# Eight batches of attention and a mixture of experts on one core: the first pair of heads in pieces, low parts on VectorE or GpSimd, and other costs and keys in the planner

## The chip, the cores and the metric

The kernel runs on one core of a Trainium2 chip. The metric is the device time of one execution in microseconds (us). A core has five engines that run beside each other, each with its own instruction stream that is worked off strictly in order: TensorE (PE in the profile, its weight loads PEld), VectorE (DVE), ScalarE (ACT), GpSimd (POOL) and SyncE (SP), which here only issues DMAs. An instruction that waits for a semaphore holds up everything behind it on its engine.

## The reference, cut to what matters

```python
def _attn_ref(q, k, v):                       # (8, 8, 576, 64) each
    ...
    q_rot, k_rot = (rotate(q), rotate(k))     # rotary embedding
    scores = scale * np.matmul(q_rot, k_rot.transpose(0, 1, 3, 2))
    scores = scores - np.max(scores, axis=-1, keepdims=True)
    attn = np.exp(scores)
    attn = attn / (np.sum(attn, axis=-1, keepdims=True) + 1e-09)
    return np.matmul(attn, v).astype(np.float32)

def _moe_ref(x, w_gate, w1, w2, capacity):    # x (8, 576, 512), capacity 128
    scores = np.einsum('bsd,d->bs', x, w_gate)
    out = x.copy()
    for b in range(B):
        top_idx = np.argpartition(-scores[b], capacity)[:capacity]
        xe = x[b, top_idx]
        h = np.maximum(xe @ w1, 0.0)          # 512 -> 1024
        ye = h @ w2                           # 1024 -> 512
        g = 1.0 / (1.0 + np.exp(-scores[b, top_idx]))
        out[b, top_idx] = x[b, top_idx] + g[:, None] * ye
    return out.astype(np.float32)
```

## The kernel before

The 64 heads are worked as 32 pairs, two heads on 64 partitions each; four pairs make a batch. For every pair SyncE loads k and q (640 KB each, every column with its rotated partner beside it) and v. `rotate` multiplies k and q in place by tables of cosines and sines (`tabk`, `tabq`) and adds the two halves, into `rk` and `rq`, 640 columns each: two multiplies of 1280 elements and two adds of 640 for a pair. `tabq` is `tabk` times 1/8, made once by ScalarE. `split_qk` splits each of `rk` and `rq` into a rounded high part (`kh`, `qh`, a cast on ScalarE) and a low part (`kl`, `ql`, the difference, "low part" below), so that three matmuls (kh·qh, kl·qh, kh·ql) give a product of nearly full precision. There is one `rk` and one `rq` for all pairs: the add of the next pair must wait until high and low part of this one are made. `k_in` and `q_in` have two buffers each.

`attend` then makes nine units of scores for a pair (two heads by 4.5 tiles of 128 rows, each 128x576 in PSUM). For each unit VectorE takes the negative row maximum (`nm`), ScalarE the exponential with row sums (`pab`, or `pr` for the last unit), TensorE turns it with transposes, ScalarE or VectorE copies the turned tile to SBUF (`pt`, `pk`), TensorE multiplies with v, and after another transpose VectorE scales the rows into `x`. Every second pair `x` is stored, and GpSimd multiplies it by the gate's weights (`prod`). When a batch is complete, `route` counts ranks on VectorE, picks 128 tokens, GpSimd gathers them, and TensorE puts them through two layers, again with three matmuls for a product. The weights of these layers are loaded in 16 pieces of 256 KB through two stages (`xe`, `row`) during the first batches and split into high (ScalarE) and low parts (GpSimd), the `w` instructions.

The first pair (`first` in `rotate`) is rotated by VectorE, all others by GpSimd. All low parts of k and q are made by VectorE, 640 columns in one instruction (the first pair's q in two pieces).

The order of every engine's stream is set on the host, before the program is built. Each piece of work is an `Op` with a key (when it is wanted) and, for each engine that may do it, how long the engine is taken and when the result is there. `Order.run` plays these Ops forward in time: an engine that is free takes the ready Op with the smallest key, TensorE also with a price for changing between three kinds of matmul (`SWITCH`), and Ops that may run on two engines go to the one that takes them first. The numbers in `KEY` are added to the keys or set limits: `ahead` is how early the split of a pair is wanted, `kstep` how much later its q comes than its k, `load` and `rotate` how early loads and rotations are wanted. An Op of `mode` 2 on VectorE begins in the plan no earlier than GpSimd is free, and GpSimd then waits for it; before the change only ten small gate products at the very end carry that mode there. All instructions go through one helper (`call`, L204 in the profile of before), so the profile's rows are told apart by the names of their tiles.

## Time and profile before

| | before |
|---|---|
| median of 3 runs (lowest to highest) | 676.64 us (676.56 to 678.98) |
| the profiled execution's own time | 677.76 us |
| its span, first to last instruction | 676.0 us |
| PE busy in the span | 622.7 us (92%) |
| DVE, ACT, POOL busy | 537.5, 419.4, 387.6 us |
| mean granted clock of TensorE | 0.988 |

A row of the timeline gives the start and the length in us, the engine, the operation, the tiles written and read, the number of instructions merged, and in brackets how long the engine had been idle before and what released it. A busy time includes the time in which an instruction that has started waits for a port. A row of the groups gives the total busy time in us and the mean of one instruction in ns.

### The profile page before, as it was taken

What the parts mean: (1) busy time and instruction counts of PE and PEld (TensorE: products, weight loads), DVE (VectorE), ACT (ScalarE), POOL (GpSimd) and SP (SyncE); (2) the same over time, 40 slices, a digit from 0 to 9 for tenths busy, and PEclk for the clock granted to TensorE, in tenths of its full rate; (3) what the DMA queues carried; (4) which work ended last, traced back from release to release, by engine and by line L of the source; (5) the groups of instructions that cost most, each with busy time, mean ns of one, the idle gap of its engine ahead of it and who ended that gap; (6) DMA issues with size and microseconds to landing.
All of it is one profiled execution on the core that took longest, in us unless ns stands there. A gap on an engine that the chain in (4) does not pass through costs nothing.

```text
span 676.0 us, 13857 instructions
## 1 busy us (share of the span) xinstructions
PE 622.7 (92%) x5072; PEld 474.5 (70%) x5072; DVE 537.5 (80%) x1294; ACT 419.4 (62%) x998; POOL 387.6 (57%) x260
## 2 busy tenths in 40 slices
PE   1789898999799999999999999999999999999896
PEld 0657676777677776787767777777777777677674
DVE  6978788899978958897787978789687978879451
ACT  3657767777566656676676656766665666757211
POOL 4877879883875656655575765557476533201110
PEclk9989999899999999999999999999999999999999
DMA  9524655331351334233233323322343302001200
GB/s 322 173 87 149 199 169 156 114 97 58 114 171 57 129 112 138 90 111 102 82 113 96 131 79 114 114 94 87 112 148 95 116 19 84 18 2 36 67 17 31
DMA packets 36708, 71.02 MB, mean 105 GB/s; under 512 B 7712, under 2 KB 25120, under 8 KB 36640
## 3 DMA queue, kind: packets, MB, share of 16 engines
q1 hardware_dynamic: 35216, 65.29, 30.2%
q0 software_dynamic: 1280, 4.20, 1.7%
q8 instruction: 40, 0.66, 0.4%
q10 hardware_dynamic: 144, 0.66, 0.3%
q14 instruction: 28, 0.23, 0.1%
HBM read 58.59 MB, written 11.53 MB: 104 GB/s over the span
## 4 chain that ended last, share of the span: by engine, by line
PE 50%; DVE 32%; issue 7%; ACT 4%; POOL 4%; DMA 2%; POOLq 0%; DVEq 0%; ACTq 0%
PE ps L204 50%; DVE nm L204 9%; DVE junk L204 6%; DVE pt L204 3%; ACT pab L204 3%; DVE ql L204 3%; DVE kl L204 2%; DVE x L204 2%; POOL prod L204 2%; DVE sel L204 1%; DVE rs L204 1%; DVE gp L204 1%; DMA k_in<-k_dram 1%; DMA row<-w_dram 1%; DMA xe<-w_dram 1%
## 5 line engine op out<-in xcount | busy, mean ns | idle before, releaser
L204 ACT ACTIVATE pab<-ps,nm 128x576 f32<-128x576 f32 x256 | 188.1, 740 | 122.5 <-DVE nm L204 121.8
L204 DVE TENSOR_REDUCE nm<-ps 128x1 f32<-128x576 f32 x288 | 205.8, 749 | 70.8 <-PE ps L204 68.6
L204 PE MATMUL ps<-ident,pab 128*128 128x128 f32 x1152 | 162.2, 281 | 13.0 <-ACT pab L204 9.0
L204 PEld LDWEIGHTS ps<-ident,pab 128*128 128x128 f32 x1152 | 132.6, 144 | 29.1 <-ACT pab L204 14.2
L204 PE MATMUL ps<-pt,vt 128*64 128x320 f32 (+1 forms) x1024 | 140.3, 417 | 0.4 <-ACT pab L204 0.4
L204 POOL TENSOR_TENSOR k_in<-k_in,tabk 128x1280 f32<-128x1280 f32 x31 | 91.0, 2937 | 50.5 <-DMA k_in<-k_dram 50.5
L204 PE MATMUL ps<-kh,qh 64*128 64x288 f32 (+1 forms) x576 | 85.7, 346 | 22.9 <-ACT qh L204 10.6
L204 ACT COPY pt<-ps 128x512 f32<-128x512 f32 x156 | 89.0, 597 | 25.5 <-PE ps L204 25.2
L204 PEld LDWEIGHTS ps<-pt,vt 128*64 128x64 f32 x1024 | 68.7, 138 | 50.1 <-issue 8.1
L204 POOL TENSOR_TENSOR rk<-k_in 128x640 f32<-128x640 f32 x31 | 60.9, 1964 | 66.6 <-DVE kl L204 54.9
L204 DVE COPY pt<-ps 128x512 f32<-128x512 f32 x132 | 88.3, 680 | 9.7 <-PE ps L204 7.1
L204 PEld LDWEIGHTS ps<-kh,qh 64*128 64x128 f32 (+1 forms) x576 | 49.1, 188 | 65.7 <-ACT pab L204 30.4
L204 POOL TENSOR_TENSOR q_in<-q_in,tabq 128x1280 f32<-128x1280 f32 x31 | 91.3, 2947 | 4.6 <-DMA q_in<-q_dram 4.4
L204 POOL TENSOR_TENSOR prod<-x,wg 128x512 f32<-128x512 f32 (+1 forms) x45 | 52.3, 1163 | 50.4 <-DVE x L204 23.0
L204 PE MATMUL ps<-kh,ql 64*128 64x288 f32 (+1 forms) x576 | 70.3, 297 | 5.5 <-DVE ql L204 5.3
L204 PE MATMUL ps<-kl,qh 64*128 64x288 f32 (+1 forms) x576 | 69.6, 295 | 0.3 <-DVE kl L204 0.3
L204 PEld LDWEIGHTS ps<-kh,ql 64*128 64x128 f32 (+1 forms) x576 | 52.6, 188 | 6.2 <-DVE ql L204 6.2
L204 PEld LDWEIGHTS ps<-kl,qh 64*128 64x128 f32 (+1 forms) x576 | 52.5, 188 | 0.6 <-DVE kl L204 0.6
L204 PE MATMUL ps<-w,xt 128*128 128x512 f32 x192 | 51.7, 409 | 1.2 <-ACT xt L204 0.6
L204 POOL TENSOR_TENSOR rq<-q_in 128x640 f32<-128x640 f32 x31 | 48.2, 1554 | 7.4 <-DVE rs L204 4.3
L204 PE MATMUL ps<-w,ht 128*128 128x512 f32 x192 | 51.3, 406 | 0.5 <-DVE ht L204 0.5
L204 ACT ACTIVATION_READ_ACCUMULATOR pab<-ps,nm 128x1 f32 x256 | 50.6, 198 | 0.0
(94 smaller groups left out, 779.7 us busy)
## 6 DMA issues: line engine op xcount, KB each, us to landing
k_in<-k_dram SPq DMA_DIRECT2D x32, 640.0 KB, 3.9
q_in<-q_dram SPq DMA_DIRECT2D x32, 640.0 KB, 5.3
vt<-v_dram SPq DMA_DIRECT2D x32, 256.0 KB, 3.1
out_dram<-x SPq DMA_DIRECT2D x16, 512.0 KB, 3.6
xe<-w_dram SPq DMA_DIRECT2D x8, 256.0 KB, 3.5
row<-w_dram SPq DMA_DIRECT2D x8, 256.0 KB, 3.4
vr<-v_dram SPq DMA_DIRECT2D x64, 16.0 KB, 2.5
out_dram<-x SPq DMA_DIRECT2D x16, 64.0 KB, 3.2
```

Source lines behind the costliest of these rows:

```text
L204: i = made(*args, **kwargs)
```

## The change

In the first pair, k is cut at column 352 and q at columns 128 and 384 (`KCUTS`, `QCUTS`). Loads, table, rotation, high and low parts are made piece by piece, the pieces of k and q in turn; the table comes in two DMAs on ScalarE's queue, now Ops of the plan. For all later pairs the low parts may be made by VectorE or GpSimd, and so may the low parts of the expert weights. In the plan, VectorE's instructions with two operands in SBUF (rotation and low parts) carry `mode` 2, and such an Op isn't taken by VectorE while GpSimd is busy. Transfers carry their bytes (`moved`) and land one after the other at 350 bytes a ns, plus 1700 ns. Three costs (row sums and reciprocals, the parts of the gate scores, the gather) are set higher, and all numbers in `KEY` but `half` and `hold` are new; two lines of them stand for the rest below.

```diff
-KEY = dict(ahead=5300, lag=11900, rem=120, value=3300, rows=13200, load=22300, rotate=92400, half=2000,
-           gate=15815, route=58400, count=31800, select=12400, turn=17500, step=9176, kstep=2700, hold=2,
...
+KEY = dict(ahead=6669, lag=12977, rem=76, value=4203, rows=388, load=49858, rotate=24073, half=2000,
+           gate=54405, route=49769, count=21851, select=23426, turn=18811, step=10093, kstep=3, hold=2,
...
+                        if e == "DVE" and o.mode == 2:
+                            can = max(can, free["POOL"])
...
+                    if o.moved:
+                        wire = max(wire, begin + takes) + o.moved / 350.0
+                        lasts = wire - begin + 1700.0
...
+    def any_of(n):
+        return {"DVE": dve(n), "POOL": pool(n)}
+
+    def engine(e):
+        return nc.vector if e == "DVE" else nc.gpsimd
...
+    KCUTS, QCUTS = (0, REM + HALF, KW), (0, P, 3 * P, KW)
...
-        dma("k", kin.tile, k[b, j], kin, 0)
-        dma("q", qin.tile, q[b, j], qin, 1)
-        dma("v", vt.tile, main(v), vt, 2)
+        for n, use, src, cuts in ("k", kin, k, KCUTS), ("q", qin, q, QCUTS):
+            for i, (lo, hi) in enumerate(zip(cuts, cuts[1:]) if pi == 0 else [(0, KW)]):
+                dma(n, use.tile[:, :, lo:hi], src[b, j, :, :, lo:hi], use, 2 * i + (n == "q"), 8 * P * (hi - lo))
+        dma("v", vt.tile, main(v), vt, 5, 8 * P * NT * D)
...
-        for name, use, r, tab, cuts in (
-            ("k", kin, rk, tabk, (0, KW)), ("q", qin, rq, tabq, (0, P, KW) if first else (0, KW))):
+        for name, use, r, tab, cuts in (("k", kin, rk, tabk, KCUTS), ("q", qin, rq, tabq, QCUTS)):
...
+            for i, (lo, hi) in enumerate(zip(cuts, cuts[1:]) if first else [(0, KW)]):
+                e = "DVE" if first else "POOL"
+                soon = 2 * i + (name == "q") if first else 0
...
+            for i, (lo, hi, o) in enumerate(made[name]):
+                if pi == 0:
+                    key = at(0, 0) - KEY["rotate"] + 2 * i + n + 0.5
...
-                d = op({"DVE": dve(hi - lo)},
-                       lambda h=h, l=l, src=src: nc.vector.tensor_tensor(l, src, h.bitcast(F32), op=ALU.subtract),
-                       key, [c] + lu.before)
+                d = op({"DVE": dve(hi - lo), **({"POOL": pool(hi - lo)} if pi else {})},
+                       lambda e="DVE", h=h, l=l, src=src: engine(e).tensor_tensor(l, src, h.bitcast(F32), op=ALU.subtract),
+                       key, [c] + lu.before, mode=2)
...
-            d = op({"POOL": pool(DM)},
-                   lambda hi=hi, lo=lo, stage=stage: nc.gpsimd.tensor_tensor(
-                       lo, stage, hi.bitcast(F32), op=ALU.subtract), key + 3000, [c])
+            d = op(any_of(DM),
+                   lambda e, hi=hi, lo=lo, stage=stage: engine(e).tensor_tensor(
+                       lo, stage, hi.bitcast(F32), op=ALU.subtract), key + 3000, [c], mode=2)
...
-    nc.scalar.dma_start(tabk, rope)
...
+    for i, (lo, hi) in enumerate(zip(KCUTS, KCUTS[1:])):
+        tab_ready["k"].append([op(
+            {"ACT": (450, 2900)}, lambda lo=lo, hi=hi: nc.scalar.dma_start(tabk[:, :, lo:hi], rope[:, :, lo:hi]),
+            at(0, 0) - 2 * KEY["rotate"], moved=8 * P * (hi - lo))])
```

What the new plan does to the streams shows at three places. The first is VectorE's start, from its first rotation (`k_in`, `q_in` are the multiplies, `rk`, `rq` the adds, `kl`, `ql` the low parts, `nm` the first row maximum). Before:

```order
L204 TENSOR_TENSOR k_in_80<-k_in_80,tabk 128x1280
L204 TENSOR_TENSOR q_in_78<-q_in_78,tabq 128x2x128
L204 TENSOR_TENSOR rk_82<-k_in_80 128x640
L204 TENSOR_TENSOR rq_83<-q_in_78 128x128
L204 TENSOR_TENSOR q_in_78<-q_in_78,tabq 128x2x512
L204 TENSOR_TENSOR kl_86<-rk_82,kh_84 128x640
L204 TENSOR_TENSOR rq_83<-q_in_78 128x512
L204 TENSOR_TENSOR ql_90<-rq_83,qh_88 128x128
L204 TENSOR_TENSOR ql_90<-rq_83,qh_88 128x512
L204 TENSOR_REDUCE nm_114<-ps_63 128x1
```

And now, from the fourth rotation on (two instructions on k's first piece and one on q's come before):

```order
L211 TENSOR_TENSOR rq_83<-q_in_78 128x128
L211 TENSOR_TENSOR k_in_80<-k_in_80,tabk 128x2x288
L211 TENSOR_TENSOR kl_86<-rk_82,kh_84 128x352
L211 TENSOR_TENSOR ql_90<-rq_83,qh_88 128x128
L211 TENSOR_TENSOR rk_82<-k_in_80 128x288
L211 TENSOR_TENSOR q_in_78<-q_in_78,tabq 128x2x256
L211 TENSOR_TENSOR kl_86<-rk_82,kh_84 128x288
L211 TENSOR_TENSOR rq_83<-q_in_78 128x256
L211 TENSOR_TENSOR q_in_78<-q_in_78,tabq 128x2x256
L211 TENSOR_TENSOR ql_90<-rq_83,qh_88 128x256
L211 TENSOR_TENSOR rq_83<-q_in_78 128x256
L211 TENSOR_REDUCE nm_114<-ps_63 128x1
```

Nine instructions stood ahead of the first maximum and fourteen smaller ones do now; the low part of q's last piece comes behind the sixth maximum.

The second place is GpSimd behind the small `tok` instructions of the first routing, where the third batch comes near. Before:

```order
L204 TENSOR_TENSOR k_in_81<-k_in_81,tabk 128x1280
L204 TENSOR_TENSOR rq_83<-q_in_79 128x640
L204 TENSOR_TENSOR prod_118<-x_109,wg 64x256
L204 TENSOR_TENSOR q_in_79<-q_in_79,tabq 128x1280
L204 TENSOR_TENSOR rk_82<-k_in_80 128x640
L204 TENSOR_TENSOR rq_83<-q_in_78 128x640
L204 TENSOR_TENSOR k_in_80<-k_in_80,tabk 128x1280
L204 TENSOR_TENSOR q_in_78<-q_in_78,tabq 128x1280
```

And now:

```order
L211 TENSOR_TENSOR rq_83<-q_in_79 128x640
L211 TENSOR_TENSOR kl_87<-rk_82,kh_85 128x640
L211 TENSOR_TENSOR ql_91<-rq_83,qh_89 128x640
L211 TENSOR_TENSOR k_in_80<-k_in_80,tabk 128x1280
L211 TENSOR_TENSOR q_in_78<-q_in_78,tabq 128x1280
L211 TENSOR_TENSOR prod_118<-x_109,wg 128x512
L211 TENSOR_TENSOR rk_82<-k_in_80 128x640
L211 TENSOR_TENSOR rq_83<-q_in_78 128x640
```

The two low parts of a pair stand between its adds and the next pair's multiplies. Over the whole stream GpSimd makes 29 of the 31 later `kl`, 25 of the 31 later `ql`, and 10 of the 16 low parts of the weights; VectorE makes the rest, 14 instructions.

The third place is SyncE's start. Before:

```order
L204 DMA k_in_80<-k_dram 128x1280
L204 DMA q_in_78<-q_dram 128x1280
L204 DMA vt_92<-v_dram 128x2x256
L204 DMA vr_95<-v_dram 64x64 x2
L204 DMA k_in_81<-k_dram 128x1280
L204 DMA q_in_79<-q_dram 128x1280
```

And now:

```order
L211 DMA k_in_80<-k_dram 128x2x352
L211 DMA q_in_78<-q_dram 128x2x128
L211 DMA k_in_80<-k_dram 128x2x288
L211 DMA q_in_78<-q_dram 128x2x256 x2
L211 DMA vt_92<-v_dram 128x2x256
L211 DMA vr_95<-v_dram 64x64 x2
L211 DMA k_in_81<-k_dram 128x1280
```

The second pair's k stands behind the same bytes as before, in three more DMAs. On TensorE the same 4432 matmuls are issued; changes between its three kinds of matmul are 253 where they were 251. From the first transposes of the last batch's gate scores (`sc`) to the end, its stream has the same matmuls, in the same order but for one transpose.

## Rows read from the trace of the kernel before

**Rows 1.** The page's first part: busy us, share of the span, instructions.

```profile
PE 622.7 (92%) x5072; PEld 474.5 (70%) x5072; DVE 537.5 (80%) x1294; ACT 419.4 (62%) x998; POOL 387.6 (57%) x260
```

**Rows 2.** Busy time by stretch of the span: the stretch and its length, then the busy us (and instructions) of each engine, the granted clock, the DMA engines' share and GB/s.

```profile
0.00:20.00 20.00, 3.69 (x22) 2.65 (x24) 13.88 (x26) 5.42 (x9) 10.84 (x23) 1.00 0.87 313
20.00:136.00 116.00, 104.14 (x873) 78.86 (x875) 94.68 (x172) 81.43 (x194) 96.69 (x52) 0.96 0.45 146
136.00:200.00 64.00, 58.60 (x519) 44.50 (x518) 58.66 (x140) 44.23 (x106) 44.10 (x28) 0.97 0.33 108
200.00:600.00 400.00, 390.92 (x3244) 298.60 (x3245) 328.57 (x798) 261.16 (x627) 226.27 (x145) 1.00 0.30 96
...
640.00:676.00 36.00, 27.48 (x130) 21.04 (x129) 13.21 (x52) 6.28 (x12) 4.01 (x8) 0.96 0.12 39
```

**Rows 3.** The timeline of the first 20 us, all engines (rows between are left out).

```profile
6.67 1.46 ACT L204 ACTIVATE tabq<-tabk 128x256 f32<-128x256 f32 x3 [4.16 <-DMA tabk<-rope_dram]
6.93 1.49 DVE L204 TENSOR_TENSOR k_in<-k_in,tabk 128x1280 f32<-128x1280 f32 x1 [3.12 <-DMA k_in<-k_dram]
8.38 0.42 DVE L204 TENSOR_TENSOR q_in<-q_in,tabq 128x256 f32<-128x256 f32 x1
...
10.55 0.85 PE L204 MATMUL ps<-kh,qh 64*128 64x288 f32 x4 [10.55 <-ACT qh L204]
...
10.92 3.44 POOL L204 TENSOR_TENSOR k_in<-k_in,tabk 128x1280 f32<-128x1280 f32 x1 [7.49 <-DMA k_in<-k_dram]
11.54 3.38 DVE L204 TENSOR_TENSOR rq<-q_in 128x512 f32<-128x512 f32 x1
...
14.33 3.33 POOL L204 TENSOR_TENSOR q_in<-q_in,tabq 128x1280 f32<-128x1280 f32 x1
14.84 4.93 DVE L204 TENSOR_TENSOR ql<-rq,qh 128x128 fp32r<-128x128 f32 x2
...
17.86 0.85 PE L204 MATMUL ps<-kh,ql 64*128 64x288 f32 x4 [5.34 <-DVE ql L204]
...
19.69 2.74 DVE L204 TENSOR_REDUCE nm<-ps 128x1 f32<-128x576 f32 x4
```

**Rows 4.** The timeline of TensorE alone: the rows with the long idle times after 20 us. Of five such rows, one in each batch from 263.76 to 576.21 (1.32, 1.33, 1.32, 1.04 and 1.33 us), the first and the last are shown.

```profile
31.11 0.40 PE L204 MATMUL ps<-kh,qh 64*128 64x288 f32 x2 [1.25 <-DVE pt L204]
40.15 0.40 PE L204 MATMUL ps<-kh,qh 128*128 128x288 f32 x1 [1.90 <-ACT pab L204]
82.65 0.48 PE L204 MATMUL ps<-ident,pab 128*128 128x128 f32 x1 [2.46 <-ACT pab L204]
118.87 0.40 PE L204 MATMUL ps<-kh,qh 64*128 64x288 f32 x2 [1.65 <-ACT w L204]
156.23 0.33 PE L204 MATMUL ps<-ident,pab 128*128 128x128 f32 x1 [1.34 <-DVE x L204]
183.74 0.33 PE L204 MATMUL ps<-ident,pab 128*128 128x128 f32 x1 [3.47 <-ACT pab L204]
263.76 0.40 PE L204 MATMUL ps<-kh,qh 128*128 128x288 f32 x1 [1.32 <-ACT pab L204]
576.21 0.40 PE L204 MATMUL ps<-kh,qh 128*128 128x288 f32 x1 [1.33 <-ACT pab L204]
```

**Rows 5.** The timeline of VectorE and GpSimd ahead of four of these idle times.

```profile
35.34 3.17 DVE L204 TENSOR_TENSOR kl<-rk,kh 128x640 fp32r<-128x640 f32 x1
...
114.48 3.58 DVE L204 TENSOR_TENSOR ql<-rq,qh 128x640 fp32r<-128x640 f32 x1
...
178.10 3.32 POOL L204 TENSOR_TENSOR q_in<-q_in,tabq 128x1280 f32<-128x1280 f32 x1
...
178.59 3.51 DVE L204 TENSOR_TENSOR ql<-rq,qh 128x640 fp32r<-128x640 f32 x1
...
260.28 1.89 DVE L204 TENSOR_TENSOR ql<-rq,qh 128x640 fp32r<-128x640 f32 x1
```

**Rows 6.** Groups of instructions with different shapes kept apart: total busy us, mean ns of one, idle time before them and its releasers.

```profile
L204 POOL TENSOR_TENSOR q_in<-q_in,tabq 128x1280 f32<-128x1280 f32 x31 | 91.3, 2947 | 4.6 <-DMA q_in<-q_dram 4.4
L204 POOL TENSOR_TENSOR rk<-k_in 128x640 f32<-128x640 f32 x31 | 60.9, 1964 | 66.6 <-DVE kl L204 54.9 <-ACT ot L204 11.7
L204 POOL TENSOR_TENSOR rq<-q_in 128x640 f32<-128x640 f32 x31 | 48.2, 1554 | 7.4 <-DVE rs L204 4.3 <-DVE ql L204 3.1
L204 DVE TENSOR_TENSOR ql<-rq,qh 128x640 fp32r<-128x640 f32 x31 | 38.7, 1248 | 0.0
L204 DVE TENSOR_TENSOR kl<-rk,kh 128x640 fp32r<-128x640 f32 x32 | 30.5, 955 | 0.0
L204 POOL TENSOR_TENSOR w<-xe,w 128x512 fp32r<-128x512 f32 x8 | 10.2, 1277 | 1.6 <-DMA row<-w_dram 1.6
L204 DVE TENSOR_TENSOR rk<-k_in 128x640 f32<-128x640 f32 x1 | 0.8, 818 | 0.0
```

**Rows 7.** The timeline of ScalarE ahead of TensorE's idle time at 80 us.

```profile
81.24 0.62 ACT L204 CAST w<-row 128x512 fp32r<-128x512 f32 x1 [2.29 <-DMA row<-w_dram]
```

**Rows 8.** Who waited for whom: engine and line, the releaser, us in total, times, longest. The first row is TensorE's matmuls, the second its weight loads.

```profile
PE ps L204 <- ACT pab L204: 18.6, 17, 3.5
...
PEld ps L204 <- ACT pab L204: 46.5, 76, 3.7
```

**Rows 9.** The chain that ended last, in order of time, where the last batch's routing begins.

```profile
639.85 1.21 PE ps L204 x9
```

More of the change, by code (lines that the diff above doesn't have):

```diff
@@ L66 @@
 class Op:
-    __slots__ = ("engines", "fn", "key", "banks", "waits", "outs", "ready", "start", "end", "done", "mode", "seq", "urgent")
+    __slots__ = ("engines", "fn", "key", "banks", "waits", "outs", "ready", "start", "end", "done", "mode", "seq", "urgent",
+                 "moved")
 class Order:
@@ L78, in __init__, with op @@
         self.ops, self.slots = [], slots
-    def op(self, engines, fn, key, after=(), bank=None, mode=0, urgent=False):
+    def op(self, engines, fn, key, after=(), bank=None, mode=0, urgent=False, moved=0):
         o = Op()
+        o.moved = moved
         o.urgent = urgent
@@ L463, in rotate, with tt @@
         made = {}
-        def tt(n, out, in0, in1, alu, after, uses):
-            e = nc.vector if first else nc.gpsimd
-            o = op({"DVE": dve(n)} if first else {"POOL": pool(n)},
-                   lambda: e.tensor_tensor(out, in0, in1, op=alu), key, after)
+        def tt(on, n, out, in0, in1, alu, after, uses, soon):
+            e = nc.vector if on == "DVE" else nc.gpsimd
+            o = op({on: dve(n) if on == "DVE" else pool(n)},
+                   lambda: e.tensor_tensor(out, in0, in1, op=alu), key + soon, after, mode=2 * (on == "DVE"))
             for u in uses:
@@ L802, in parts @@
             nc.gpsimd.tensor_tensor(cols[2], r1.tile, cols[1], op=ALU.subtract)
-        o = op({"POOL": (500, 500)}, parts, key, [s] + tk.before + r1.before)
+        o = op({"POOL": (1030, 1030)}, parts, key, [s] + tk.before + r1.before)
         sc.by(o), tk.by(o), r1.by(o)
```

44 lines of the change are left out of this document (24 added, 20 removed).

## The prediction

> **What bounds the kernel now.** I read the page's busy times first: TensorE is busy for 622.7 of 676.0 us, VectorE for 537.5, GpSimd for 387.6 [rows 1]. So the end is set by TensorE's work plus its idle time, 53.4 us, and a change that leaves TensorE's work alone can win little more than that. The stretches say where the idle time lies [rows 2]: 16.3 us in the first 20 us, 11.9 us from 20 to 136, 5.4 us from 136 to 200, 9.1 us from 200 to 600, 8.5 us after 640, and the rest, 2.2 us, between. The granted clock is 0.96 to 1.00 in all of them, so the clock isn't the subject.
>
> Next I read the start instruction by instruction [rows 3]. TensorE begins at 10.55, stops for 5.34 us, and the first row maximum comes only at 19.69. VectorE is the cause, and what holds it is GpSimd: its add `rq` of 512 elements starts at 11.54 and lasts 3.38 us, until just after GpSimd's multiply (10.92 to 14.36) has ended, though the add of 640 elements takes 0.82 us when nothing is beside it [rows 6]. Then the two low parts of q take 4.93 us while GpSimd's next multiply runs from 14.33 to 17.66. So an instruction of VectorE with two operands in SBUF and one of GpSimd don't run at once: the later one waits for the whole of the other.
>
> Then I went to TensorE's long idle times later on [rows 4] and looked at what VectorE did just before each. Ahead of the 1.90 us at 40 stands a `kl` of 3.17 us, ahead of the 1.65 us at 118 a `ql` of 3.58 us, ahead of the 3.47 us at 183 one of 3.51 us beside a multiply of GpSimd, ahead of the 1.32 us at 263 one of 1.89 us [rows 5]. Behind it VectorE's row maximum is late, then the exponential, then the transposes. The idle times at 31 and 156 have a `ql` ahead of them too, and the four later ones like that at 263 come once in each batch. The one of 2.46 us at 82 is another thing: ScalarE's cast of a weight piece waits 2.29 us for its load and holds up the exponentials behind it [rows 7].
>
> **The change part by part.** The sum is made against the profiled execution's own time, 677.76 us, of which 676.0 are span; the median of the runs is 676.64, so 1.1 us come off at the end.
>
> *The start.* VectorE's first multiply needs two pieces of 352 columns instead of two whole 640 (k and the table). That is 2 x 288 columns x 8 bytes x 128 partitions = 590 KB less ahead of it; at the 313 GB/s of this stretch [rows 2] 1.9 us, so it starts at about 5.05 instead of 6.93. Fourteen instructions with 4864 elements now stand ahead of the first maximum. A multiply of 1280 takes 1.49 us and one of 256 takes 0.42 [rows 3], so 1.04 ns for an element; with some 0.1 us for each instruction that is 6.5 us, and VectorE would be done at 11.6. GpSimd's first multiply still starts when the second pair's k has landed, and as many bytes stand ahead of that as before: about 10.9. So the last one to three of the fourteen meet it. If none waits, the first maximum comes at 11.7; if one does, at 14.6 (2.95 us for a multiply, rows 6); if two do, with the second multiply between them, at 17.6. Against 19.69 that is -8.0, -5.1 or -2.1. I take the middle one. The worst end is +2: pieces that land no sooner, and three waits.
>
> [...]
>
> *Low parts that leave VectorE.* 29 `kl` of 0.955 us and 25 `ql` of 1.248 us [rows 6] are 58.9 us; six low parts of weights, some 0.7 us each by the 0.82 us for 640 elements, come to it. VectorE falls from 537.5 to about 483 us. What counts is the idle time that they caused on TensorE: 1.25 + 1.90 + 1.65 + 1.34 + 3.47 = 9.6 us in five places, and 6.3 us in the five later batches [rows 4], together 15.9. With the low part gone from VectorE there is no wait ahead of the maximum. Six `ql`, two `kl` and six weight pieces stay with VectorE, most of them before 200 us, each able to wait up to 2.95 us. So of 15.9 I take -13; the ends are 0 and -16.
>
> *Weight pieces.* Their loads begin earlier in the new stream and are spread wider; the 2.46 us [rows 4] should go for the most part: -2, ends 0 and -2.5.
>
> *Idle time that the busy time hides.* TensorE's weight loads waited 46.5 us for the exponentials, its matmuls only 18.6 [rows 8]; the other 27.9 us lie under ends of matmuls that the profile models, and part of them is the change from one kind of matmul to another, which stays (253 for 251). VectorE's shorter queue may win some of it. Ends 0 and -14; I take -3, near the end that the trace shows outright.
>
> *What GpSimd gets.* 54 low parts of 1.554 us, as its add of the same size that rarely waits (`rq`), are 83.9 us; six weight pieces of 1.277 leave, 7.7 us; and its adds into `rk` stop waiting for VectorE's low parts, (1.964 - 1.554) x 31 = 12.7 us [rows 6]. 387.6 + 83.9 - 7.7 - 12.7 = 451 us, 69% of the new span. That is hidden behind TensorE unless a low part stands behind a multiply of 2.95 us when TensorE wants it. From 20 to 136 GpSimd is already busy for 96.7 of 116 us [rows 2], so there it has little room. I take +1, ends 0 and +10.
>
> *The tail.* From the transposes of the last gate scores at 639.85 [rows 9] to the end it is 36 us of the same work: 0.
>
> *Smaller things.* The raised costs and the other keys change only the order; that has no price of its own, and I count it in the terms above.
>
> Sum: -5.1 - 13 - 2 - 3 + 1 = -22.1. 677.8 - 22.1 = 655.7, and 1.1 less for the median: 654.5 us.
>
> **The rivals.**
>
> *GpSimd becomes the bound in the first 200 us.* For it: 83% busy from 20 to 136, and a pair brings 54 / 31 x 1.554 = 2.7 us more, some 17 us for the six or so pairs of that stretch, while the weight pieces take only 7.7 away: about 106 of 116 us if nothing got shorter. Then the early idle times (9.6) and the 2 us of the weights stay under another name, and the hidden time isn't won: -5.1 - 6.3 = -11.4, so 665. Against it: 12.7 us of that busy time were waits for VectorE. The Trainium skill, page "Perfetto Trace Analysis", section "Optimizing Scalar/DVE Operations", says that GpSimd and VectorE share a read port of SBUF, so moving work between them might not help. The trace agrees on the port; the rule would have the low part hold it for 1.55 us instead of 0.8. It leaves out that the one who waited here was the engine ahead of the exponentials.
>
> *The regained time is lost again.* TensorE is 98% busy from 200 to 600 [rows 2]; where one wait goes, the next one (bank free, exponential) can end as late. Then only the start stays: -5, 671.5. For it: the idle times in the rows are short beside the 78 us of a batch (576.21 - 263.76, over four, rows 4). Against it: VectorE loses a tenth of its work, so the next wait is shorter too.
>
> *Slower: the low parts come too late.* Two low parts on GpSimd take 3.1 us in a row where VectorE needed about 1.6, and a multiply of 2.95 us may stand ahead of them. If they hold up the scores of a pair by t us, 31 pairs cost 31 t against the 7 us won at the start and the weights and what is left of the low parts' 13; it decides from t = 0.65 us if those 13 are won, and from 0.23 if not. At one us in most pairs, with the 13 lost: -7 + 25 = +18, 695. For it: the adds into `rk` already waited 54.9 us for `kl` [rows 6], so the chain through the single `rk` is tight. Against it: after 200 GpSimd is busy for only 226 of 400 us [rows 2], and the splits are wanted 1.4 us (k) and 4.1 us (q) sooner in the new keys.
>
> *Better than I think.* No wait at the start (-8), all 15.9 and 2.5, the hidden time at -14: -40, 636.
>
> **How the numbers follow.** Forecast, 648 to 662: 0.54. GpSimd the bound, about 665: 0.15. Lost again, about 671.5: 0.12. Too late, 680 to 700: 0.09. Better: 0.10. About 0.5% (3.4 us) is what a measurement of this kernel can tell from no change, so faster means below 673.3. Faster gets the forecast, the first and the last rival and two thirds of the second: 0.86, of which I give 0.01 away, 0.85; within 0.5% the rest of the second and a part of the third: 0.07; slower 0.08. The range leaves out the third rival and the outer half of the last: 640 to 672.
>
> **What the profile afterwards would show.** Right: VectorE's first multiply near 5 us and the first maximum between 11.5 and 17.6; `kl` and `ql` on GpSimd near 1.55 us; idle times of TensorE over 1 us after 200 us gone; VectorE near 483 and GpSimd near 450 us busy; the 36 us from the gate scores to the end as before. Wrong: TensorE's weight loads or matmuls released by `kl` or `ql` on GpSimd, or ScalarE's casts waiting for `rk` or `rq`, in most pairs; VectorE's few low parts near 3 us ahead of a row maximum; a start at 19 us as before.

## The result and the profile after

The changed kernel takes 647.62 us (median of 4 runs, 647.53 to 648.06), the kernel before 676.60 (median of 4 runs). The ratio is 0.9566, 95% interval 0.9544 to 0.9589: 29 us less. The forecast was 654.5 in a range of 640 to 672. The profiled execution took 648.06 us, with a span of 646.3 against 676.0.

The page's first part of after, beside [rows 1]:

```profile
PE 610.5 (94%) x5072; PEld 470.4 (73%) x5072; DVE 492.8 (76%) x1264; ACT 413.6 (64%) x989; POOL 447.2 (69%) x308
```

TensorE's idle time in the span fell from 53.4 to 35.9 us, and its busy time by 12.2 with the same 5072 matmuls. So 17.5 us of the 29.7 are idle time that one could see before, and 12.2 had been counted as busy. (The trace has 5072 rows for the 4432 matmuls that are issued: by the counts, each of the 640 with v stands in it as two.) To see where, I cut both spans at the same work: at the start of the first row maximum (`nm`) of pair 0, of pair 12 and of pair 28, and at the first transpose of the last gate scores (`sc`). Busy time by these stretches (columns as in [rows 2]), of before:

```profile
0.00:19.70 19.70, 3.50 (x20) 2.47 (x20) 13.58 (x26) 5.42 (x9) 10.75 (x22) 1.00 0.89 318
19.70:237.30 217.60, 199.82 (x1681) 151.90 (x1683) 186.91 (x409) 150.04 (x355) 163.69 (x95) 0.97 0.39 126
237.30:549.80 312.50, 305.25 (x2538) 233.31 (x2540) 257.03 (x625) 204.60 (x492) 190.80 (x117) 1.00 0.33 105
549.80:639.85 90.05, 86.45 (x707) 65.62 (x706) 66.77 (x185) 53.06 (x130) 18.30 (x20) 1.00 0.11 33
639.85:676.05 36.20, 27.63 (x130) 21.19 (x130) 13.21 (x52) 6.28 (x12) 4.08 (x8) 0.96 0.12 39
```

And of after:

```profile
0.00:11.80 11.80, 2.59 (x18) 2.24 (x20) 7.03 (x31) 4.35 (x9) 2.67 (x20) 1.00 0.83 288
11.80:223.70 211.90, 197.10 (x1702) 151.09 (x1702) 176.39 (x407) 147.10 (x351) 191.84 (x113) 0.99 0.43 143
223.70:524.70 301.00, 299.78 (x2538) 232.21 (x2538) 233.24 (x597) 204.09 (x491) 228.56 (x148) 1.00 0.34 110
524.70:609.01 84.31, 82.31 (x693) 62.87 (x693) 62.68 (x180) 51.72 (x126) 20.03 (x22) 1.00 0.11 35
609.01:646.32 37.31, 28.67 (x130) 21.98 (x130) 13.47 (x52) 6.33 (x12) 4.08 (x8) 0.94 0.11 38
```

The first number is the length, the second TensorE's busy time, their difference its idle time. The start gives 7.9 us, the first three batches 5.7, the four steady batches (pair 12 to 28) 11.5, the last batch's attention 5.7, and the tail costs 1.1. In the steady batches idle time fell from 7.25 to 1.22 and busy time from 305.25 to 299.78, with 2538 matmuls in either.

Part of the rest is TensorE's clock. In the first three batches the granted clock (the column after the engines) is 0.97 before and 0.99 after. Before, four stretches of 3.4 us there show 0.50, the lower level of 1.2 GHz; each begins within 1.6 us of the end of an idle time of [rows 4] (those before 40.15, 82.65, 118.87 and 183.74). After, one does, behind the idle time of 3.49 us shown further down. Two of the four, and the one:

```profile
41.70:45.10 3.40, 3.40 (x14) 1.57 (x16) 2.15 (x6) 1.19 (x3) 1.34 (x1) 0.50 0.01 2
185.00:188.50 3.50, 3.50 (x21) 2.64 (x21) 2.23 (x8) 1.70 (x4) 2.64 (x4) 0.51 0.96 278
89.00:92.50 3.50, 3.50 (x22) 2.98 (x20) 1.74 (x5) 1.85 (x5) 3.50 (x3) 0.51 0.45 152
```

The price can be read from the tail, which is nearly the same work in all kernels below. Where the clock stays at its upper level until the last 3 us, the tail takes 36.1 to 36.4 us (before and five runs); with 3.4 us at the lower level 37.3 (after and one run); with 6.8 us 38.2 to 38.9 (six runs). So 3.4 us at the lower level cost about 1 us there. That is the whole of the tail's 1.1 us. For the first three batches, three such stretches fewer are some 3 us of their 5.7, by an estimate from the tail; it is at most 5.0, half of the difference in busy time at that level (13.6 us before, 3.5 after).

The start, in the timeline of after (rows between are left out), beside [rows 3]:

```profile
5.51 0.89 DVE L211 TENSOR_TENSOR k_in<-k_in,tabk 128x704 f32<-128x704 f32 x1 [1.71 <-DMA k_in<-k_dram]
...
8.09 0.61 PE L211 MATMUL ps<-kh,qh 64*128 64x288 f32 x2 [8.09 <-ACT qh L211]
...
11.46 0.41 DVE L211 TENSOR_TENSOR rq<-q_in 128x256 f32<-128x256 f32 x1
11.57 3.07 POOL L211 TENSOR_TENSOR k_in<-k_in,tabk 128x1280 f32<-128x1280 f32 x1 [8.15 <-DMA k_in<-k_dram]
...
11.80 2.74 DVE L211 TENSOR_REDUCE nm<-ps 128x1 f32<-128x576 f32 x4
```

None of the fourteen pieces waits: VectorE's last add starts 0.11 us before GpSimd's first multiply. The multiply also starts 0.65 us later than before; SyncE, with three more DMAs to issue ahead of it, issues its load at 6.25 us instead of 3.82.

Of TensorE's idle times of over 1.3 us after the start, one is left before 600 us. It lasts 3.49 us and comes in the same way as in [rows 5]: VectorE's low part of a weight piece starts behind GpSimd's multiply, and row maximum and exponential are late by it.

```profile
82.31 2.91 POOL L211 TENSOR_TENSOR k_in<-k_in,tabk 128x1280 f32<-128x1280 f32 x1
82.53 3.25 DVE L211 TENSOR_TENSOR w<-row,w 128x512 fp32r<-128x512 f32 x1
85.18 3.35 POOL L211 TENSOR_TENSOR q_in<-q_in,tabq 128x1280 f32<-128x1280 f32 x1
85.70 2.74 DVE L211 TENSOR_REDUCE nm<-ps 128x1 f32<-128x576 f32 x4
86.54 0.74 ACT L211 ACTIVATE pab<-ps,nm 128x576 f32<-128x576 f32 x1 [3.81 <-DVE nm L211]
87.42 0.66 PE L211 MATMUL ps<-ident,pab 128*128 128x128 f32 x4 [3.49 <-ACT pab L211]
```

The groups of after, beside [rows 6]:

```profile
L211 POOL TENSOR_TENSOR rk<-k_in 128x640 f32<-128x640 f32 x31 | 49.8, 1606 | 0.3
L211 POOL TENSOR_TENSOR kl<-rk,kh 128x640 fp32r<-128x640 f32 x29 | 45.1, 1555 | 55.7 <-ACT kh L211 55.6
L211 POOL TENSOR_TENSOR ql<-rq,qh 128x640 fp32r<-128x640 f32 x25 | 39.8, 1590 | 4.8 <-ACT qh L211 4.8
```

`rk` no longer waits for VectorE's `kl` (54.9 us before); GpSimd now waits as long for ScalarE's cast `kh`, but the chain that ended last has 0% of the span on GpSimd. And who waited for whom, beside [rows 8]:

```profile
PEld ps L211 <- ACT pab L211: 34.6, 58, 3.7
...
PE ps L211 <- ACT pab L211: 13.1, 14, 3.5
```

### The profile page after: what moved, and what is told of

It reads as the page before. It is cut to its first block, busy times and chain, and to the rows that moved or that the text cites. A ratio compares the mean times of both kernels' runs of the same rounds, so it can differ in the third digit from the quotient of the medians.

```text
span 646.3 us, 13873 instructions
## 1 busy us (share of the span) xinstructions
PE 610.5 (94%) x5072; PEld 470.4 (73%) x5072; DVE 492.8 (76%) x1264; ACT 413.6 (64%) x989; POOL 447.2 (69%) x308
## 4 chain that ended last, share of the span: by engine, by line
PE 72%; DVE 16%; issue 6%; ACT 3%; DMA 1%; POOL 0%; POOLq 0%; DVEq 0%; ACTq 0%; SPq 0%
PE ps L211 72%; DVE nm L211 5%; DVE junk L211 4%; ACT pab L211 2%; DVE pt L211 2%; DVE x L211 1%; DVE w L211 1%; DMA k_in<-k_dram 1%; DMA xe<-w_dram 1%; DVE ql L211 0%; DVE row L211 0%; DVE ht L211 0%; DVE rs L211 0%; DVE pk L211 0%; DVE gp L211 0%
## 5 line engine op out<-in xcount | busy, mean ns | idle before, releaser
L211 PE MATMUL ps<-pt,vt 128*64 128x320 f32 (+1 forms) x1024 | 138.2, 412 | 0.9 <-DVE pk L211 0.9
L211 POOL TENSOR_TENSOR k_in<-k_in,tabk 128x1280 f32<-128x1280 f32 x31 | 90.6, 2923 | 21.5 <-DMA k_in<-k_dram 21.4
L211 DVE COPY pt<-ps 128x512 f32<-128x512 f32 x132 | 86.9, 680 | 6.5 <-PE ps L211 6.2
L211 POOL TENSOR_TENSOR kl<-rk,kh 128x640 fp32r<-128x640 f32 x29 | 45.1, 1555 | 55.7 <-ACT kh L211 55.6
L211 POOL TENSOR_TENSOR prod<-x,wg 128x512 f32<-128x512 f32 (+1 forms) x45 | 49.0, 1088 | 25.8 <-DVE gp L211 18.9
```

Source lines behind the costliest of these rows:

```text
L211: i = made(*args, **kwargs)
```

## The experiments

Theory: the gain has two sources, the start (the pieces) and VectorE's freedom from waits for GpSimd (the low parts moved). Main rival: the new keys or the planner's new rules carry it, and the moved low parts alone give little or cost something. Below, "issued" means that the stream's order stays and only the engine changes; "planned anew" means that the planner ran again, so that the whole order can differ. The stages are those above; the column "rest" joins the last batch's attention with the tail.

| kernel | first maximum | first 3 batches | 4 steady batches | rest | median of runs | ratio to before (95%) |
|---|---|---|---|---|---|---|
| before | 19.7 | 217.6 | 312.5 | 126.2 | 676.6 | 1 |
| after | 11.8 | 211.9 | 301.0 | 121.6 | 647.62 | 0.9566 (0.9544 to 0.9589) |
| after, low parts issued on VectorE | 12.7 | 246.7 | 310.2 | 121.1 | 692.95 | 1.0245 (1.0207 to 1.0283) |
| before, low parts issued on GpSimd | 19.5 | 223.7 | 312.1 | 128.4 | 687.06 | 1.0165 (1.0124 to 1.0206) |
| after, weights issued on GpSimd | 11.8 | 215.2 | 301.1 | 122.5 | 651.3 | 0.9622 (0.9582 to 0.9663) |
| after, start made late | 14.9 | 211.9 | 300.9 | 122.7 | 651.53 | 0.9618 (0.958 to 0.9657) |
| after, all low parts issued on GpSimd | 12.1 | 209.6 | 301.2 | 120.8 | 645.19 | 0.9535 (0.9507 to 0.9563) |
| the same kernel again | 12.4 | 209.6 | 301.1 | 120.8 | 646.45 | 0.9557 (0.9531 to 0.9583) |
| after, old keys | 11.9 | 221.9 | 308.4 | 128.4 | 672.3 | 0.9923 (0.99 to 0.9946) |
| before, new keys | 19.5 | 219.5 | 304.8 | 123.2 | 669.86 | 0.9905 (0.9873 to 0.9937) |
| after, plan blind to the shared access | 12.2 | 225.0 | 301.1 | 120.5 | 660.89 | 0.9766 (0.9738 to 0.9793) |
| after, first pair uncut | 15.4 | 223.8 | 300.6 | 122.5 | 662.78 | 0.9773 (0.9732 to 0.9813) |
| after, loads not by bytes | 11.9 | 240.4 | 300.3 | 120.4 | 674.31 | 0.9955 (0.9936 to 0.9973) |
| after, old gate key | 11.9 | 218.5 | 304.6 | 122.4 | 658.73 | 0.973 (0.9704 to 0.9756) |

In the rounds of these runs the kernel before took 676.1 to 677.3 us (medians), so rows that differ by about 1 us aren't told apart. A plan made anew also changes the order in places that the edit doesn't touch: in all five variants of after that were planned anew the first three batches take 6.6 to 28.5 us more than after's 211.9, even where only one key was put back. So what such a run loses there can't be put down to the edited part alone. The four steady batches suffer less from this: in three of the five they take 300.3 to 301.1 us, as after.

### The low parts alone, from both sides

After's order, with the 54 later low parts of k and q that its plan gave to GpSimd issued on VectorE:

```diff
-                       lambda e="DVE", h=h, l=l, src=src: engine(e).tensor_tensor(l, src, h.bitcast(F32), op=ALU.subtract),
+                       lambda e="DVE", h=h, l=l, src=src: nc.vector.tensor_tensor(l, src, h.bitcast(F32), op=ALU.subtract),
```

> The changed kernel's plan is kept, every stream as it is, but the 54 low parts of k and q that it gives to GpSimd are issued by VectorE at the same places. If the gain between 20 and 610 us comes from VectorE no longer waiting for GpSimd's instructions ahead of a row maximum, the low parts come back with 0.8 to 3.5 us each, VectorE's busy time goes from 493 to over 540 us, and the time to 662 us or more. If the gain is the new keys' order alone, the time stays within 3 us of 647.6.

692.95 us, 45 more than after. The groups of this run:

```profile
L211 DVE TENSOR_TENSOR kl<-rk,kh 128x640 fp32r<-128x640 f32 x31 | 42.5, 1370 | 0.0
L211 POOL TENSOR_TENSOR rk<-k_in 128x640 f32<-128x640 f32 x31 | 48.7, 1571 | 87.2 <-DVE kl L211 87.1
```

Low parts on VectorE meet GpSimd again, and `rk` waits 87.1 us for them. In this plan the move matters much; but the order counts on it, so 45 us is no measure of what the move is worth elsewhere.

Before's order, with all 62 later low parts issued on GpSimd:

```diff
-                       lambda h=h, l=l, src=src: nc.vector.tensor_tensor(l, src, h.bitcast(F32), op=ALU.subtract),
+                       lambda h=h, l=l, src=src: (nc.gpsimd if pi else nc.vector).tensor_tensor(l, src, h.bitcast(F32), op=ALU.subtract),
```

> The old kernel's plan is kept, every stream as it is, but the low parts of k and q of all pairs after the first (62) are issued by GpSimd at the same places. If the waits of VectorE are the cause, TensorE's idle times at 31, 40, 118, 156, 184 and once per batch go and the time falls by 10 to 16 us, to 661 to 667. If low parts on GpSimd come too late unless the plan knows of them, the time is 676 or more and TensorE waits for kl or ql in most pairs.

687.06 us, slower than before. VectorE falls to 477.4 us busy and no low part waits there any more, yet the four steady batches take 312.1 us as before (312.5). The timeline shows what took the lock's place, once per batch (rows between left out):

```profile
270.42 1.55 POOL L204 TENSOR_TENSOR rq<-q_in 128x640 f32<-128x640 f32 x1
...
271.93 0.72 POOL L204 TENSOR_TENSOR prod<-x,wg 64x256 f32<-64x256 f32 x1
272.68 0.41 DVE L204 TENSOR_REDUCE gp<-prod 64x1 f32<-64x256 f32 x1 [2.74 <-POOL prod L204]
...
273.21 1.42 DVE L204 TENSOR_REDUCE nm<-ps 128x1 f32<-128x576 f32 x2
...
274.89 0.53 PE L204 MATMUL ps<-kh,qh 64*128 64x288 f32 x4 [1.54 <-ACT pab L204]
```

GpSimd's gate product stands behind the low part and the adds; VectorE's sum of it, `gp`, waits 2.74 us with the row maxima queued behind, and TensorE idles 1.54 us where it had idled 1.32 [rows 4].

What it loses lies elsewhere: of the 7.7 us by which its span is longer, 6.1 are in the first three batches and 2.2 behind pair 28. In the first batches three idle times of TensorE (3.44, 3.54 and 2.08 us, at 69, 84 and 105) come where ScalarE's cast of a weight piece waits for its load and holds up the exponentials, as in [rows 7]:

```profile
67.88 0.62 ACT L204 CAST w<-xe 128x512 fp32r<-128x512 f32 x1 [4.01 <-DMA xe<-w_dram]
69.28 0.85 PE L204 MATMUL ps<-kh,qh 64*128 64x288 f32 x4 [3.44 <-ACT pab L204]
```

So the time is as the second expectation has it, but its reason didn't come: behind the first pair TensorE waits for no `kl` or `ql` on GpSimd. The move by itself wins nothing; the order has to be made for it.

### Keys against everything else

After's code with before's keys, planned anew, and before's code with after's keys, planned anew (the diff of the second is that of the first, turned round):

```diff
-KEY = dict(ahead=6669, lag=12977, rem=76, value=4203, rows=388, load=49858, rotate=24073, half=2000,
...
+KEY = dict(ahead=5300, lag=11900, rem=120, value=3300, rows=13200, load=22300, rotate=92400, half=2000,
...
```

> The changed kernel with all the numbers in KEY as they were before, planned anew: pieces, low parts on either engine, port and bytes known to the plan. If the engine of the low parts and the plan's knowledge carry the gain, 650 to 660. If the new keys carry it, 668 or more, with waits of row maxima behind sums of gate products that GpSimd makes too late, as in the old plan with low parts on GpSimd.

> The old kernel with the new numbers in KEY alone, planned anew, low parts all on VectorE. If low parts on VectorE are what costs, it stays at 674 or more, with low parts of 1.2 us and more on average. If the keys alone carry the gain, 655 to 665.

672.3 and 669.86 us: each half alone gives 4 to 7 us, together they give 29. (The first time is as the expectation has it for the keys; the second lies between the two that were expected.) The stages divide it. The start belongs to the new code (11.9 with old keys; 19.5 with new keys alone). In the steady batches the keys alone give 7.7 of 11.5 us, with all low parts still on VectorE, and the new code alone 4.1. By the same stretches, TensorE is idle for 8.1 of 308.4 us with old keys (0.87 and 1.00 us once per batch in two new places), and for 3.4 of 304.8 with new keys alone, against 7.25 before and 1.22 after. In the steady batches of before's code with new keys the long `ql` still stands on VectorE once per batch, with 1.28 us for 1.89. In the first three batches neither half alone gives anything (221.9 and 219.5 for 217.6); there it takes both.

One key alone, when the gate's work of a batch is wanted, put back in after and planned anew:

```diff
-           gate=54405, route=49769, count=21851, select=23426, turn=18811, step=10093, kstep=3, hold=2,
+           gate=15815, route=49769, count=21851, select=23426, turn=18811, step=10093, kstep=3, hold=2,
```

> The kernel after with one number of the planner's keys put back: when the gate's products and scores of a batch are wanted (15815 instead of 54405), planned anew. With all keys put back the four steady batches took 77.1 us each instead of 75.3. Theory (this key alone carries the steady gain, since with the old one GpSimd's product and VectorE's sums of it stand ahead of row maxima once per batch): steady batches 76.5 to 77.1 us, 652 to 660 us. Rival (the steady gain comes from when splits and loads are wanted, ahead and kstep): steady batches 75.0 to 75.6 us, 645 to 652 us.

76.15 us for a steady batch, between the two expectations: 0.9 of the 1.85 us by which all old keys lengthen it (77.1 against 75.25). TensorE then idles 0.93 us once per batch, ahead of the first expert layer (the first of four such rows):

```profile
259.96 1.66 PE L211 MATMUL ps<-w,xt 128*128 128x512 f32 x6 [0.93 <-ACT pab L211]
```

The steady batches make 3.6 of the 11.1 us by which this run is slower than after; 6.6 lie in the first three batches. The other half of the steady gain wasn't divided further among the remaining keys, and the three raised costs weren't tested by themselves.

### What the planner knows

The planner not told that VectorE's rotations and low parts share their access with GpSimd, planned anew:

```diff
-                   lambda: e.tensor_tensor(out, in0, in1, op=alu), key + soon, after, mode=2 * (on == "DVE"))
+                   lambda: e.tensor_tensor(out, in0, in1, op=alu), key + soon, after)
...
-                       key, [c] + lu.before, mode=2)
+                       key, [c] + lu.before)
...
-                       lo, stage, hi.bitcast(F32), op=ALU.subtract), key + 3000, [c], mode=2)
+                       lo, stage, hi.bitcast(F32), op=ALU.subtract), key + 3000, [c])
```

> The changed kernel, planned anew without the knowledge that VectorE's instructions with two operands in SBUF and GpSimd's exclude each other (no mode 2 on rotations and low parts). The plan then gives 38 instead of 54 low parts of k and q to GpSimd. If the knowledge matters, VectorE's low parts last 1.5 us and more on average, idle times of 1 to 3.5 us stand behind them in every batch, and the time is 660 to 680. If it doesn't, 645 to 651.

660.89 us, in the range for a knowledge that matters, but not in its way: the steady batches stay at 301.1, without idle times behind low parts, though 16 fewer of them are on GpSimd. The first three batches take 225.0 us for 211.9. The plan now takes VectorE for 14 of 16 weight pieces, as if it could start them at any time, and they wait, lasting 1.80 us on average:

```profile
40.69 3.52 POOL L211 TENSOR_TENSOR q_in<-q_in,tabq 128x1280 f32<-128x1280 f32 x1
41.94 2.82 DVE L211 TENSOR_TENSOR w<-xe,w 128x512 fp32r<-128x512 f32 x1
...
48.00 0.55 PE L211 MATMUL ps<-ident,ot 128*128 128x128 f32 x3 [3.65 <-ACT pab L211]
```

The planner without the bytes of transfers, planned anew:

```diff
-                    if o.moved:
+                    if False:
```

> The kernel after, planned anew with transfers costed as before the change (each with a length of its own, none behind another); everything else is as after. Theory (the bytes matter only where loads are dense, in the first 140 us, and there little, since the keys already ask for loads early): first maximum within 1 us of after's 11.8, pair 0 to pair 12 within 4 us of 211.9, four steady batches 301 as after, 646 to 652 us. Rival (the plan without the bytes believes loads of k, q and weight pieces to land together and puts instructions that need them ahead of work that is ready): engines wait for loads in the first 140 us, 216 to 226 us in that stretch, 652 to 662 us; steady batches as after.

674.31 us: the kind of the rival, and more than it asked for. The steady batches take 300.3 us, the first three 240.4, 28.5 more than after's. TensorE's idle time there is 38.15 us for 14.80, of which three idle times make 28.1; the other 5.2 us are busy time, at a granted clock of 0.94 for 0.99. One of the three is 4.38 us at 137, behind a `ql` of 7.05 us on VectorE; the other two are larger. For one, ScalarE's cast of a weight piece stands ahead of the exponentials and waits for its load, so that TensorE idles 8.76 us before 20.63. The rows show this cast and then the third idle time:

```profile
18.51 0.62 ACT L211 CAST w<-xe 128x512 fp32r<-128x512 f32 x1 [8.29 <-DMA xe<-w_dram]
...
80.56 17.00 DVE L211 TENSOR_TENSOR w<-row,w 128x512 fp32r<-128x512 f32 x1
81.26 1.55 POOL L211 TENSOR_TENSOR kl<-rk,kh 128x640 fp32r<-128x640 f32 x1
...
94.13 2.87 POOL L211 TENSOR_TENSOR k_in<-k_in,tabk 128x1280 f32<-128x1280 f32 x1
...
98.01 0.90 PE L211 MATMUL ps<-ident,ot 128*128 128x128 f32 x3 [14.92 <-DVE ot L211]
```

One low part of VectorE takes 17.00 us: it started while GpSimd was in an add, and eight more GpSimd instructions went past it until GpSimd had nothing to do at 97.0. TensorE idles 14.92 us behind it. The cast that waits 8.29 us for its load is what the rival named. That the long low parts come from the missing bytes too, and not from the chance of a new plan, isn't shown.

### The start

After with the first pair cut as before, planned anew:

```diff
-    KCUTS, QCUTS = (0, REM + HALF, KW), (0, P, 3 * P, KW)
+    KCUTS, QCUTS = (0, KW), (0, P, KW)
```

> The kernel after with the first pair cut as before (k whole, q at column 128 only), planned anew; everything else is as after. Theory (the 7.9 us won at the start come from the pieces, and a shift of the start goes through to the end, as with the late start): first row maximum near 19 us, the stages behind it as after but for a few us of plan noise, 652 to 660 us. Rival A (the start is early because the plan now knows the shared access and lets the first maximum go ahead of the later rotations, and the pieces matter little): first maximum near 13 to 15, 648 to 652 us. Rival B (the finer start also orders the first batches well): the stretch from the first maximum to pair 12's is longer than after's 211.9 by 5 us or more, 660 to 668 us.

First maximum at 15.4, 662.78 us. Of the 7.9 us at the start 4.3 come without the pieces, because the first two maxima now go ahead of the add and the low part of q's second piece. The pieces are worth the other 3.6 here. In this run the low part of q's first piece starts at 11.52, 0.21 us behind GpSimd's first multiply, and lasts 2.97 us; in after the last piece starts 0.11 us ahead of it. The first three batches take 223.8 us for 211.9, as rival B said: in the new order low parts left on VectorE wait 6.35 us (`kl` at 92.31) and 5.53 (`ql` at 148.39) for GpSimd. I read these 11.9 us as the chance of a new plan, not as a price of whole pieces; no run here separates the two.

After's order with a clear of 128x256 elements put ahead of the low part of q's second piece, so that the last of the fourteen instructions, an add, comes behind the start of GpSimd's first multiply:

```diff
+                           late and nc.vector.memset(hs_.tiles[0][:, 0:256], 0.0),
```

> The changed kernel with one more small instruction on VectorE (a memset of 128x256, about 0.3 us) ahead of the low part of the second piece of the first pair's q. In the changed kernel the last of the fourteen instructions began 0.1 us before GpSimd's first multiply (11.46 and 11.57). If two engines exclude each other for a whole instruction, that last one now waits for the multiply and the first row maximum moves from 11.8 to about 15. If what is won at the start goes through to the end, the time rises by 2.5 to 3.5 us, to 650 to 651; if later slack takes it up, it stays under 648.6.

651.53 us. The add lasts 3.11 us for 0.41, the first maximum comes at 14.9 instead of 11.8, and the two middle stages keep their length (211.9 and 300.9): 3.1 us later at the start are 2.9 us later at pair 28. The run is another 1.1 us longer behind that, in the tail, where 6.8 us at the lower clock stand for 3.4. A shift of the start goes through, and the start's 7.9 us count in full. With the wait, the pieces bring the first maximum only 0.5 us ahead of the uncut run's 15.4: most of their 3.6 us is that they slip past the multiply.

### The low parts that VectorE kept

After's order with the six weight pieces of VectorE issued on GpSimd:

```diff
-                   lambda e, hi=hi, lo=lo, stage=stage: engine(e).tensor_tensor(
+                   lambda e, hi=hi, lo=lo, stage=stage: nc.gpsimd.tensor_tensor(
```

> The changed kernel's plan is kept, but the six low parts of weights that it gives to VectorE are issued by GpSimd at the same places. In the changed kernel they last 1.6 to 3.3 us on VectorE and TensorE's idle times of 1.26, 1.10 and 3.49 us at 48, 65 and 87 us follow such an instruction. If their wait is the cause, the time falls by 3 to 6 us, to 642 to 645. If GpSimd is the bound before 136 us (87% busy there), six more instructions of 1.28 us on it make the early pairs later, and the time is 648 or more.

651.3 us, 3.7 more than after, by one instruction:

```profile
78.27 1.29 POOL L211 TENSOR_TENSOR w<-xe,w 128x512 fp32r<-128x512 f32 x1
...
78.45 10.18 DVE L211 TENSOR_TENSOR kl<-rk,kh 128x640 fp32r<-128x640 f32 x1
79.50 1.55 POOL L211 TENSOR_TENSOR ql<-rq,qh 128x640 fp32r<-128x640 f32 x1
...
88.68 0.61 PE L211 MATMUL ps<-kl,qh 64*128 64x288 f32 x2 [7.45 <-DVE kl L211]
88.77 1.55 POOL L211 TENSOR_TENSOR rk<-k_in 128x640 f32<-128x640 f32 x1 [0.83 <-DVE kl L211]
```

`kl` on VectorE lasts 10.18 us, past five GpSimd instructions in a row, and ends only when the next of them, `rk`, has to wait for it.

The same, with the eight later low parts of k and q that VectorE had kept moved as well, so that after the first pair no low part is left on VectorE:

```diff
-                       lambda e="DVE", h=h, l=l, src=src: engine(e).tensor_tensor(l, src, h.bitcast(F32), op=ALU.subtract),
+                       lambda e="DVE", h=h, l=l, src=src: (nc.gpsimd if pi else nc.vector).tensor_tensor(l, src, h.bitcast(F32), op=ALU.subtract),
...
-                   lambda e, hi=hi, lo=lo, stage=stage: engine(e).tensor_tensor(
+                   lambda e, hi=hi, lo=lo, stage=stage: nc.gpsimd.tensor_tensor(
```

> The changed kernel's plan is kept, but all low parts behind the first pair, those of k, q and the weights, are issued by GpSimd at the places the plan has for them. In the run with only the weights moved, one kl left on VectorE lasted 10.2 us and TensorE stood still for 7.5 us at 81. If VectorE's waits are what is left to win before 136 us, both this and the idle times of 1.1 to 3.5 us in the changed kernel go and the time is 641 to 646. If GpSimd is the bound there, the 14 more instructions on it (some 20 us of work) make the early pairs later: 650 or more.

645.19 us. The next expectation takes this run for one with the eight low parts alone, which it isn't; no run has them alone. The kernel is the same again:

> The plan of the kernel after, with all later low parts of k and q and all low parts of the weights issued on GpSimd (14 instructions more than after there). After the first pair no instruction of VectorE then needs the access that GpSimd holds, but for ten small products at the very end. Alone, the six weight pieces cost 3.7 us, by one low part of VectorE that waited 10.18 us; alone, the eight low parts won 2.4 us. Theory (what the weights cost on GpSimd was that one wait, and with the low part gone from VectorE it goes): no idle time of TensorE over 2.3 us before 200 us, 642 to 646 us. Rival (GpSimd is too full in the first 140 us, 101 of 116 us busy after, and 14 instructions of 1.3 to 1.6 us more make its rotations late): idle times of TensorE of 3 us and more behind rotations or low parts there, 648 to 655 us.

646.45 us. In both, the first three batches take 209.6 us for 211.9, and the longest idle time of TensorE after the start is 2.2 us, at 103. In both, the clock keeps its upper level until the last 3 us. In the second run GpSimd is busy for 112.13 of the 116 us from 20 to 136 (columns as in [rows 2]), and from 40 to 60 and 80 to 100 without a break:

```profile
20.00:136.00 116.00, 103.83 (x931) 78.01 (x932) 91.25 (x214) 82.50 (x197) 112.13 (x70) 1.00 0.46 148
...
100.67 0.69 DVE L211 TENSOR_REDUCE gp<-prod 128x2 f32<-128x512 f32 x1 [3.25 <-POOL prod L211]
103.00 0.44 PE L211 MATMUL ps<-ident,ot 128*128 128x128 f32 x2 [2.23 <-ACT pab L211]
```

The longest idle time follows a `gp` that waits 3.25 us for GpSimd's `prod`. So GpSimd is full there and begins to set the pace, without the 3 us and more that the rival expected. The weight pieces cost 3.7 us while a low part stood on VectorE to be passed over; moved together with the eight low parts, they cost nothing that shows. The eight runs, 644.75 to 647.48, all lie below after's lowest, but the intervals of the ratios overlap: it is the best version here, by 1.2 to 2.4 us that these runs don't settle.

## Why the prediction was right, and where it was not

The time, 647.62, lies in the range and 6.9 below the forecast. The forecast's sum of -22.1 became -29.7 in the span. The start took 2.8 more off than forecast, the visible idle time 3.5 less, and the busy time behind the start fell by 8.3 more. These errors partly cancel, so it is in part luck that the time came as near as it did.

*The start, -5.1.* It became -7.9. The working gave -8.0 for no wait, and none came; I took one wait. That none came is luck: it was decided by 0.11 us, and the late start shows the other outcome, 3.1 us. Half of the cause was not in my working: by the uncut run 4.3 us are the new order of maxima and rotations.

*Low parts -13, weights -2, GpSimd's extra +1.* Together -14 of visible idle time; after the start it fell by 10.5. The size is near, the cause was not. I put the 6.3 us once per batch down to `ql` waiting for GpSimd. With the low parts moved and the old order, the steady batches gained 0.4 us, since `gp` behind GpSimd's `prod` was late next; with the new keys and the low parts still on VectorE they gained 7.7. So "the raised costs and the other keys change only the order; that has no price of its own" is the step that failed: in the steady batches the order carries most of what I gave to the low parts. And from 20 to 200 us, where most of the 9.6 lay, the idle time fell little: 17.8 to 14.8 us in the first three batches, since waits for GpSimd's turn went to another place. One of the signs of being wrong that I had named, a low part of about 3 us on VectorE ahead of a row maximum, came once (3.25 us at 82.53, ahead of the 3.49 us).

*Hidden idle time, -3.* This term was mis-sized: busy time fell by 12.2 us, 0.9 of it at the start and 5.5 in the steady batches with equal matmuls. The truth lies near the end at -14; the choice "near the end that the trace shows outright" was wrong. Three things are in the 12.2. What I had in mind, the weight loads' waits for exponentials less those of the matmuls, fell from 27.9 us [rows 8] to 21.5 (34.6 less 13.1), by 6.4. The clock is the second, 3 to 5 us in the first three batches by the estimate above. I had put it aside with "so the clock isn't the subject"; but it fell right behind idle times that the change was to remove, so these cost more than their length. The rest stays open, and no run tests the three by themselves.

*GpSimd's and VectorE's load.* Forecast 451 and 483, measured 447.2 and 492.8; low parts on GpSimd 1.555 and 1.590 us for 1.554.

*The tail, 0.* From the gate scores 37.31 us for 36.20, by the clock.

*The chances.* The chances of a faster kernel add up to 0.87 and not to 0.86; the stated 0.85 then gives 0.02 away.

*The rivals.* GpSimd as the bound didn't come in after (101.3 of 116 us busy); in the best version it is 112.13 and close to it. The regained time lost again, and low parts too late: neither came in after. Before's order with the low parts on GpSimd did get slower, 687.06, but through `gp` and the casts of weight pieces rather than through the scores of every pair. That is the answer to the Trainium skill's rule too. The Trainium skill, "Perfetto Trace Analysis", "Optimizing Scalar/DVE Operations", says that work moved between engines on one port might not help: it didn't with the old order (1.0165); in the order made for it, moving it back cost 45 us. The Trainium skill, "Perfetto Trace Analysis", "DMA Optimizations", says that splitting a DMA into smaller chunks may allow some to start sooner. The trace agrees: with the DMA engines 83% busy in the first 11.8 us, the first multiply, which needs one piece of k and of the table, started 1.42 us sooner (5.51 for 6.93; 6.96 in the uncut run), for the 1.9 us of my working.

## What to carry to other kernels

A move of work off a loaded engine is worth what the order around it lets through: test the move in the old order and the new order without the move before crediting either. When two engines share an access, an instruction left on one of them can be passed over for a long time; here the version that kept VectorE free of it behind the first pair was the best, by a little. Idle time once per batch has several causes of nearly the same length; remove the named one in an experiment before counting it as won. Look at the granted clock behind each idle time before calling the clock no subject. And a planned order that is made anew moves much that the edit doesn't name: to price one part, keep the order where it can be kept.

## What the runs showed of the hardware

I had expected a VectorE instruction with two operands in SBUF to wait for one GpSimd instruction, as in [rows 5]. It can wait for many: 10.18 us past five, 17.00 us past nine (the one in progress and eight behind it). In these two it ended when GpSimd waited or had nothing to do. In after, at 85.18, it got its turn between two GpSimd instructions that stood back to back. What decides between the two is open.

A long wait also costs the clock. Behind the 14.92 us idle time of the run without bytes, the windows show the granted clock at 0.50, which is the lower level of 1.2 GHz, and at 1.00 from 104 us on:

```profile
83.00:98.00 15.00, 0.09 (x1) 0.00 (x0) 15.00 (x3) 0.59 (x1) 14.00 (x7) 0.57 0.14 53
98.00:101.00 3.00, 2.99 (x14) 2.99 (x15) 2.83 (x6) 1.55 (x4) 0.00 (x0) 0.50 0.81 282
101.00:104.00 3.00, 3.00 (x25) 2.83 (x25) 1.53 (x6) 1.90 (x4) 0.00 (x0) 0.78 0.61 236
104.00:107.00 3.00, 3.00 (x32) 1.88 (x30) 2.37 (x5) 1.99 (x6) 0.00 (x0) 1.00 0.02 7
```

In the first of these 3 us stretches TensorE, busy throughout, gets 14 matmuls done, in the third 32 (of a partly other mix). Far shorter idle times of the kernel before were followed by the lower level as well, as shown with the result. What decides isn't shown: behind the 1.65 us at 118 of before the clock falls, behind the 2.2 us at 103 of the run with all low parts on GpSimd it doesn't.
